# Attention, gated MLP and mixer in one kernel: gate weights prepared during the attention, part of the last matrix stored off the chip, norm steps regrouped

## The chip, the cores and the metric

The kernel runs on one core of one Trainium2 chip. The time is the device time of one execution in microseconds (us). Before the change three runs took 1237.75, 1238.79 and 1238.87 us; their median, 1238.79, is the time before.

## The reference

Three computations follow each other on a batch of 4 (head dimension 64, 8 heads, 1152 positions, so 576 pooled positions of 512 features):

```
attention:  q' = mean over pairs of positions of q          # 4 x 8 x 576 x 64
            p  = softmax(q' k^T / 8);   x = p v              # -> x: 4 x 576 x 512
gated MLP:  h  = gelu(x w_in); u, v = halves of h            # w_in 512 x 1024
            v  = (v - mean) / sqrt(var + 1e-6) * g_ln        # norm over 512 features
            v  = w_sg v + b_sg                               # w_sg 576 x 576, over positions
            x  = x + (u * v) w_out                           # w_out 512 x 512
mixer:      u  = x + (relu(x^T w_tok1) w_tok2)^T             # over positions, 576 -> 256 -> 576
            out = u + relu(u w_ch1) w_ch2                    # over features, 512 -> 1536 -> 512
```

The matrices w_in, w_out, w_tok1, w_tok2, w_ch1 and w_ch2 arrive as 64-bit floats; w_sg arrives in 32 bits. The kernel turns each 64-bit number into a 32-bit one by integer operations on its two halves.

## The kernel before

Every matrix product is done in three passes: each operand is split into a high part, rounded to the type fp32r, and a low part, the rest, and the products high·high, high·low and low·high are summed (`PASSES`, `products`). So each weight needs a conversion and a split before its first use. One *piece* is 128 x 512 numbers (512 KB in 64 bits). `convert` (line 216) loads it into a tile `ws` (two buffers), then does four DVE steps (L239, L243, L247, L252, tile `wz`), two ACT steps before the last of them (L230, L231, tile `wd`), the copy to the high part on POOL (`g_scale`, L210) and the subtraction for the low part on POOL (`sub`, L214). The class `Feed` holds a queue of such pieces; each call of `feed.ops(1)` issues one of the four steps. `Feed.add` appends pieces and starts the first two loads at once; `feed.until(n)` issues whatever is missing until n pieces are done.

The order of all instructions is written out by the program; each engine executes its own list in order.

*Attention* (lines 329 to 701). Sixteen pairs (batch, two heads). For each pair: q and k are loaded, transposed on PE, split (q on L400 to L422, k on L432 and L214); 15 score products `s` (L462) give row maxima on DVE (L469); then 18 transposed score products `sT` (L513), exponentials on ACT (L521) into eight buffers `e`, their running sum `acc` on POOL (L527), the products with v (L536, three column groups at a time), the sum over keys on PE (L549), reciprocal on DVE (L560) and the multiplication into `xT` (L567). The three PSUM banks of `s` and `sT` are shared. The order comes from the class `Plan`: tasks with an engine, a duration, an urgency, predecessors and rings of buffers are scheduled by a list simulation, and the instructions are issued in the resulting order. Sixteen planned DVE tasks call `feed.ops(1)`: with them the four pieces of the second half of w_in (`w0`) are converted during the attention. Loads of q, k and v are two half loads each, the second planned after the first has landed.

*Gated MLP* (`spatial`, from line 717 on). Per batch: V (the v half, three tile pairs, L807), norm (`v_norm`, a list of small steps: a guess, three Newton steps, then for each of five tiles `apply` on DVE and `split` on ACT and POOL), O (output product of the batch before, L915), U (the u half, four blocks, L873), S (the gate over positions, four blocks, L891). A group of products in S is followed by L900 on DVE, L903 on POOL, and a split. The table `HOOKS` says what other work is issued at each point: "0U1e" is batch 0, stage U, block 1, and a letter m, a, e or z for the place within it (in the middle of the products, after them, in the middle of the activation, at its end). The work letters are: c one conversion step, n one norm step, x the split of one tile of x, t and s steps of w_sg's preparation, f a step of closing the attention, w the adding of w_in's first half.

Before the first U stage, w_in's first half (`w1`, four pieces) is converted, since U needs it; during the stages V, U and S of batch 0, w_sg (loaded into `gu` and `b_bc`, lines 757 and 758) is split (L761, ACT and POOL), transposed in both parts by 45 PE transposes (L771), and copied out by ACT (L780, L782); and w_out (`wo`, four pieces) is converted. `bias_load` then loads b_sg and g_ln and scales them on POOL.

*Mixer* (`mixing`, from line 1034 on). F is the last output product; K and Q are the two products over positions (L1088, L1098); M and N are the first block of 256 rows of the two products over features (L1151, L1171), during which `HOOKS` still issues conversions; eight further blocks follow without any. In the last gate stage and in F, K and Q the pieces of w_ch1 (12), w_tok1 and w_tok2 (6) and the first third of w_ch2 (4) are converted; the other eight pieces of w_ch2 are added behind them and are converted in M and N, where `feed.until` makes a product wait for its piece.

Of the kernel before, what the change touches and what calls it, by code (L numbers as in the profile page):

```python
# [27 lines left out]
EARLY_ON = "PP"  # L28
YT = ((), (0, 1, 2), (3, 4), (), (), ())
HOOKS = {  # L30
# [26 lines left out]
class Plan:  # L57
# [20 lines left out]
    def run(self):  # L78
# [21 lines left out]
        while any(todo.values()):  # L100
            best = None
            for eng, ts in todo.items():
                now = free.get(eng, 0.0)
                could = []
                for t in sorted(ts, key=lambda t: t["urgency"])[:90]:
                    at = ready(t)
                    if at is not None:
                        could.append((max(at, now), t["urgency"], t["n"], t))
# [1124 lines left out]
```

## Time and profile before

| | before |
|---|---|
| median of 3 runs | 1238.79 us |
| profiled execution | 1238.36 us |
| span of the profile | 1236.5 us |
| PE busy | 1162.6 us (94%) |
| PE weight loads | 949.0 us (77%) |
| DVE busy | 711.1 us (58%) |
| POOL busy | 611.5 us (49%) |
| ACT busy | 458.5 us (37%) |
| mean granted TensorE clock | 0.978 |

The engines are PE (TensorE), DVE (VectorE), ACT (ScalarE), POOL (GpSimd) and SP (SyncE, which only issues transfers here). The page cuts the span in 40 slices of 30.9 us, one digit each, in tenths of busy time:

```profile
PE   3899999999999999998579999979989999999998
DVE  4767767776676666643976464799987112121111
ACT  1244454445444444453552423434433111111111
POOL 1477877877777777786473414263365111100100
PEclk9899999999999999998789999989998999999999
```

Slices 1 to 18 are the attention, 18 to 25 the four batches of the gated MLP, 26 to 30 the stages F, K, Q, M and N, and the rest the repeating blocks of the mixer. A digit is a mean: a wait shows in PE's row only where it is long against 31 us. Where PE is at 9, other engines' idle time costs nothing.

### The profile page before, as it was taken

Reading aid. Unit: us, or ns where it says so; the run is one execution under the profiler, and the core shown is the slowest. Engines: PE = TensorE matmul, PEld = TensorE weight load, DVE = VectorE, ACT = ScalarE, POOL = GpSimd, SP = SyncE. Lnnn points to the kernel's source line nnn. Section 1 sums busy time; section 2 is a strip of 40 time slices with the busy share of each in tenths; the row PEclk is TensorE's granted clock in tenths of the full one; section 3 lists DMA queues with packets and bytes.
Section 4 is the critical chain, followed back from the end, with each engine's and each line's share of the span. In section 5 each row is a group of like instructions: output and inputs, shape, how many; then the busy total and the mean of one; then the engine's idle time right before and its main releaser. Section 6 shows DMA issues by size and latency. Waiting matters only on the chain.

```text
span 1236.5 us, 22054 instructions
## 1 busy us (share of the span) xinstructions
PE 1162.6 (94%) x9269; PEld 949.0 (77%) x9269; DVE 711.1 (58%) x1017; ACT 458.5 (37%) x847; POOL 611.5 (49%) x452
## 2 busy tenths in 40 slices
PE   3899999999999999998579999979989999999998
PEld 2577777777767777765569898968877899999887
DVE  4767767776676666643976464799987112121111
ACT  1244454445444444453552423434433111111111
POOL 1477877877777777786473414263365111100100
PEclk9899999999999999998789999989998999999999
DMA  6412222222122211002220000023232000000000
GB/s 149 94 40 59 59 56 58 59 59 59 44 55 59 52 46 39 21 1 77 69 62 17 1 1 1 18 69 111 88 100 86 10 17 10 17 18 18 18 17 18
DMA packets 63332, 57.32 MB, mean 46 GB/s; under 512 B 39936, under 2 KB 51968, under 8 KB 63232
## 3 DMA queue, kind: packets, MB, share of 16 engines
q1 hardware_dynamic: 62176, 54.85, 16.3%
q8 instruction: 73, 1.20, 0.4%
q10 hardware_dynamic: 1056, 1.05, 0.3%
q14 instruction: 27, 0.22, 0.1%
HBM read 51.17 MB, written 4.72 MB: 45 GB/s over the span
## 4 chain that ended last, share of the span: by engine, by line
PE 37%; DVE 10%; ACT 1%; issue 1%; POOL 1%; DVEq 0%; ACTq 0%; POOLq 0%
PE psc L1151 11%; PE po L1171 11%; PE pss L891 5%; PE psv L807 3%; DVE wz L247 2%; PE psu L873 2%; PE psz L915 2%; DVE wz L243 2%; DVE wz L252 1%; DVE wz L239 1%; DVE y L214 1%; PE pso L915 1%; PE pu L1163 1%; DVE xT L1102 1%; PE psh L1098 0%
## 5 line engine op out<-in xcount | busy, mean ns | idle before, releaser
L527 POOL TENSOR_TENSOR acc<-acc,e 128x576 f32<-128x576 f32 x224 | 319.7, 1427 | 83.6 <-ACT e L521 65.2
L469 DVE TENSOR_REDUCE mx<-s 128x2 f32<-128x768 f32 (+1 forms) x240 | 225.8, 950 | 115.1 <-PE s L462 111.9
L521 ACT ACTIVATE e<-sT 128x576 f32<-128x576 f32 x288 | 184.2, 652 | 180.0 <-PE sT L513 172.9
L462 PE MATMUL s<-k,q 64*128 64x384 f32 (+1 forms) x1440 | 178.7, 351 | 2.5 <-DVE mx L469 1.9
L513 PE MATMUL sT<-q,k 64*128 64x288 f32 x1728 | 177.3, 307 | 2.6 <-DVE mx L469 1.9
L513 PEld LDWEIGHTS sT<-q,k 64*128 64x128 f32 x1728 | 135.4, 185 | 44.3 <-issue 34.5
L536 PE MATMUL po<-e,vn 128*64 128x288 f32 x1152 | 160.1, 413 | 0.0
L1151 PEld LDWEIGHTS psc<-x,w 128*128 128x128 f32 x1296 | 156.8, 190 | 3.3 <-DVE gc L1078 2.5
L1151 PE MATMUL psc<-x,w 128*128 128x256 f32 x1296 | 157.1, 283 | 2.3 <-DVE gc L1078 2.3
L1171 PE MATMUL po<-w,gc 128*128 128x512 f32 x648 | 156.4, 401 | 2.3 <-POOL w L214 1.7
L1171 PEld LDWEIGHTS po<-w,gc 128*128 128x128 f32 x648 | 121.8, 189 | 32.9 <-POOL w L214 2.5
L462 PEld LDWEIGHTS s<-k,q 64*128 64x128 f32 (+1 forms) x1440 | 116.3, 178 | 19.0 <-issue 10.3
L1077 ACT ACTIVATE gc<-psc 128x256 fp32r<-128x256 f32 x108 | 41.0, 384 | 229.9 <-PE psc L1151 229.9
L536 PEld LDWEIGHTS po<-e,vn 128*64 128x64 f32 x1152 | 75.3, 136 | 60.8 <-issue 20.1
L1078 DVE SCALAR_TENSOR_TENSOR gc<-psc,gc 128x256 fp32r<-128x256 f32 x108 | 45.5, 424 | 100.2 <-ACT gc L1077 100.2
L210 POOL TENSOR_SCALAR x<-xT 128x1024 fp32r<-128x1024 f32 x9 | 9.6, 1069 | 173.6 <-PE psc L1151 173.2
L1178 DVE TENSOR_TENSOR ob<-po,us 128x512 f32<-128x512 f32 x18 | 12.4, 691 | 133.5 <-PE po L1171 133.5
L513 PE MATMUL sT<-nmT,pick 64*128 64x288 f32 x576 | 88.2, 290 | 0.0
L560 DVE RECIPROCAL den<-den 128x288 f32<-128x288 f32 x32 | 62.3, 1947 | 35.6 <-ACT den L556 35.6
L891 PE MATMUL pss<-wsg,vn 128*128 128x288 f32 x448 | 74.6, 315 | 1.8 <-POOL vn L214 1.8
L891 PEld LDWEIGHTS pss<-wsg,vn 128*128 128x128 f32 x448 | 63.9, 193 | 12.0 <-issue 5.4
L873 PE MATMUL psu<-x,w 128*128 128x288 f32 x384 | 56.0, 307 | 10.1 <-issue 8.6
(117 smaller groups left out, 1519.0 us busy)
## 6 DMA issues: line engine op xcount, KB each, us to landing
ws<-in_moe_w_ch_dram SPq DMA_DIRECT2D x24, 512.0 KB, 3.5
qn<-in_q_dram SPq DMA_DIRECT2D x32, 288.0 KB, 4.4
kn<-in_k_dram SPq DMA_DIRECT2D x32, 288.0 KB, 4.1
vn<-in_v_dram SPq DMA_DIRECT2D x32, 288.0 KB, 3.2
out_dram<-ob SPq DMA_DIRECT2D x18, 256.0 KB, 2.0
ws<-in_moe_w_in_dram SPq DMA_DIRECT2D x6, 512.0 KB, 4.7
ws<-in_moe_w_out_dram SPq DMA_DIRECT2D x4, 512.0 KB, 3.5
gu<-in_moe_w_sg_dram SPq DMA_DIRECT2D x1, 1152.0 KB, 5.8
```

The lines of the kernel that those rows point to most:

```text
L462: nc.tensor.matmul(ps[0:m, h, 0:KC], flat(c.q[x])[r, t * P:t * P + m], c.k[y][r, cs], start=(n == 0), stop=(n == 2))
L469: nc.vector.tensor_reduce(out=mx[i % 2][0:m, t, :, g], in_=ps[0:m, :, 0:KC], axis=AX.X, op=ALU.max, negate=True)
L513: nc.tensor.matmul(ps[:, h, 0:TC], left, right, start=(n == 0), stop=(n == 3))
L521: nc.scalar.activation(out=s.e[j], in_=ps[:, :, 0:TC], func=AF.Exp)
L527: eng.tensor_tensor(out=s.acc, in0=s.e[0] if j == 1 else s.acc, in1=s.e[j], op=ALU.add)
L536: nc.tensor.matmul(s.po[D * h:D * h + D, 0:TC], c.vn[:, h, j], s.e[j][:, h], start=(j == 0), stop=(j == J - 1))
L560: nc.vector.reciprocal(out=s.den, in_=s.den)
L873: nc.tensor.matmul(ps[:, ch, 0:TC], wiu[sw][:, cc, fb * P:(fb + 1) * P], X[sx][:, cc, ch * TC:(ch + 1) * TC], start=first, stop=end)
L891: nc.tensor.matmul(ps[:, ch, 0:TC], V[sx][r, ti, db * P:(db + 1) * P], L.ws[sw][r, ti, ch * TC:(ch + 1) * TC], start=first, stop=end)
L1078: nc.vector.scalar_tensor_tensor(out=l_, in0=ps, scalar=0.0, in1=f32(h_), op0=ALU.max, op1=ALU.subtract)
L1151: nc.tensor.matmul(ps, WC1[f // 4][sw][:, cc, (f % 4) * P:(f % 4 + 1) * P], u[sx][:, cc], start=first, stop=end)
L1171: nc.tensor.matmul(pos[tt], g[sx][:, f, tt * P:(tt + 1) * P], WC2[f // 4][sw][:, f % 4], start=(f == 0 and n == 0), stop=(f == NF - 1 and ...
```

## The change

Conversion becomes a class `Piece`, whose steps can be issued by `Feed` as before or as planned tasks. The high part is now copied by ACT, not POOL. A piece has either a destination in SBUF (`dst`) or a place in device memory (`away`): then both parts are written into the piece's own `ws` tile and stored from there.

During the attention the planner now places, besides the four pieces of `w0`, the four of `w1`, the five row tiles of w_sg (unsplit PE transposes, ACT copy, DVE subtraction, stores) and the four pieces of w_out, one of these every 25 us of planned time from 60 on, each load placed behind a score product that is planned 40 us or more earlier. The two half loads of q, k and v are one task, issued together. The last group of products with v of the last pair, with its sums, reciprocal and multiplication, is marked `late` and issued through the f hooks in the first V stage of batch 0. The x splits of the first two tiles move to 40 tasks before the attention's end and, like all x splits of batch 0, to DVE. `w1`, the gate's weights and w_out are fetched back by plain loads when their SBUF space is open, and `bias_load` follows there. The conversions of eight pieces of w_ch2 (blocks 1 and 2 of 0 to 2) are issued by c hooks in the S stages of batches 0, 1 and 2 and stored; they are fetched back ahead of M. Norm steps of batch 0 stand in pairs in its U stage. The t, s and w hooks and the functions they called are gone. In the hooks from the last U stage on, the letters are unchanged.

```
-EARLY_ON = "PP"
+EARLY_ON = "DD"
 HOOKS: ...
+    "0V0a": "f", "0V0z": "f", "0V1a": "f",
+    "0U0a": "nn", "0U0e": "nn", "0U0z": "nn", "0U1a": "nn", "0U1e": "nn", "0U1z": "nn", "0U2a": "nn",
+    c in 0S: 12, in 1S: 12, in 2S: 8
...
+        def high(self):
+            if self.dst:
+                self.parts = self.dst()
+                for x in self.parts[2:]:
+                    g_scale(x, self.z, 1.0)
+            else:
+                self.parts = [self.cut(x) for x in halves(self.s)]
+            nc.scalar.copy(self.parts[0], self.z)
+        def low_part(self):
+            sub(nc.gpsimd, self.parts[1], self.z, f32(self.parts[0]))
+        def send(self, s):
+            nc.sync.dma_start(out=self.away[s], in_=f32(self.parts[s]))
...
+    def fetch(to, x):
+        for s in range(2):
+            nc.sync.dma_start(out=f32(to[s]), in_=x[s])
...
-                first = plan.add("SP", 0.05, lambda: f(i, 0, *a), urgency=u, take=[ring], land=3.5)
-                return first, plan.add("SP", 0.05, lambda: f(i, 1, *a), after=[first], urgency=u,
-                                       land=3.5)
+                return [plan.add("SP", 1.0, lambda: (f(i, 0, *a), f(i, 1, *a)), urgency=u,
+                                 take=[ring], land=4.0)]
...
-        for n in range(4 * CC):
-            plan.add("DVE", 0.75, lambda: feed.ops(1), urgency=20.0 + 26.0 * n)
-        feed.add(*row_block(0, w_in[:, DH:2 * DH], 0))
+        def conversion(x, u):
+            a = plan.add("SP", 0.05, lambda: x.load(nc.sync), after=[mark(u)], urgency=u - 20,
+                         take=["ws"], land=4.0)
+            d1 = plan.add("DVE", 1.2, x.step1, after=[a], urgency=u, take=["wz"])
+            e = plan.add("ACT", 1.4, x.early, after=[a], urgency=u, take=["wd"])
+            d2 = plan.add("DVE", 1.3, x.step2, after=[d1], urgency=u + 0.5)
+            d3 = plan.add("DVE", 1.3, x.step3, after=[d2], urgency=u + 1)
+            d4 = plan.add("DVE", 1.3, x.step4, after=[d3, e], urgency=u + 1.5, ...)
+            h = plan.add("ACT", 0.65, x.high, after=[d4], urgency=u + 2)
+            l_ = plan.add("POOL", 1.4, x.low_part, after=[h], urgency=u + 2, give=[("wz", d1)])
+            if x.away:
+                for s in range(2):
+                    plan.add("SP", 0.05, lambda s=s: x.send(s), after=[h, l_][s:s + 1], ...)
...
+        todo = [w0_piece(j) for j in range(CC)] + col_pieces(A.w1, w_in, 0)
+        todo += list(range(NTT)) + col_pieces(A.wo, w_out, 0)
+        for n, x in enumerate(todo):
+            u = 60.0 + 25.0 * n
+            if isinstance(x, int):
+                gate_weights(x, u)
+            else:
+                conversion(x, u)
+        for n in (1, 2):
+            feed.add(*row_pieces(A.c2[n], w_ch2, 512 * n))
...
         def finish():
-            yield lambda: None
-            yield lambda: None
+            yield lambda: [f() for f in rest[:-2]]
+            yield lambda: [f() for f in rest[-2:]]
             yield lambda: a2.close()
...
+            for s in range(2):
+                nc.sync.dma_start(out=f32(L.ws[s][:, 0:CC]), in_=A.ws[s][:, 0:CC])
+                for r in range(0, P, TAIL):
+                    nc.sync.dma_start(
+                        out=f32(L.ws[s][r:r + TAIL, CC:NTT]), in_=A.ws[s][0:TAIL, CC:NTT])
+            fetch(L.wo, A.wo)
+            bias_load()
...
-            return [lambda ti=ti: x_split(b, ti, nc.gpsimd)
+            return [lambda ti=ti: x_split(b, ti, nc.gpsimd if b else nc.vector)
...
-            feed.add(*row_block(i, w_ch2, 512 * (i - 4)))
+            fetch(W[i], A.c2[i - 4])
```

## Rows read from the trace of the kernel before

**Rows 1.** Stretches (us): busy time and count of each engine, clock, DMA share, GB/s

```profile
120.00:240.00 120.00, 119.39 (x1219) 86.90 (x1219) 84.20 (x110) 58.98 (x109) 93.64 (x64) 1.00 0.22 57
...
652.90:707.60 54.70, 54.70 (x354) 50.05 (x353) 28.34 (x50) 19.09 (x30) 20.81 (x17) 1.00 0.00 1
...
865.00:904.60 39.60, 37.59 (x215) 30.83 (x213) 38.53 (x54) 18.21 (x30) 16.54 (x17) 1.00 0.31 94
...
910.40:953.10 42.70, 38.14 (x226) 32.78 (x225) 36.04 (x49) 15.85 (x30) 25.12 (x22) 0.94 0.27 87
```

**Rows 2.** Timeline of the start: start, length, engine, line, operation [idle before]

```profile
0.73 0.86 SPq L221 DMA_DIRECT2D ws<-in_moe_w_in_dram  x2
...
2.88 1.87 SPq L379 DMA_DIRECT2D vn<-in_v_dram  x2
...
5.35 0.60 SPq L379 DMA_DIRECT2D kn<-in_k_dram  x1
...
15.48 1.09 PE L432 MATMUL pt<-ident,kn 128*128 128x128 f32 x4 [15.48 <-DMA kn<-in_k_dram]
```

**Rows 3.** DMA issues: count, KB each, median us from issue to landing

```profile
ws<-in_moe_w_out_dram SPq DMA_DIRECT2D x4, 512.0 KB, 3.5
gu<-in_moe_w_sg_dram SPq DMA_DIRECT2D x1, 1152.0 KB, 5.8
...
b_bc<-in_moe_w_sg_dram SPq DMA_DIRECT2D x1, 144.0 KB, 5.7
```

**Rows 4.** Groups by line and shape in the attention: busy us, mean ns

```profile
L252 DVE SCALAR_TENSOR_TENSOR wz<-wd,wz 128x512 f32<-128x512 f16 x3 | 6.3, 2097 | 0.0
...
L243 DVE SCALAR_TENSOR_TENSOR wz<-ws,wz 128x512 int32<-128x512 int32 x3 | 4.6, 1523 | 0.0
...
L247 DVE SCALAR_TENSOR_TENSOR wz<-ws,wz 128x512 int32<-128x512 int32 x3 | 2.7, 895 | 0.0
...
L239 DVE TENSOR_SCALAR wz<-ws 128x512 int32<-128x512 int32 x3 | 2.0, 663 | 0.0
```

**Rows 5.** Timeline within the attention, at its end, and at the gate's start

```profile
300.19 0.66 PE L432 MATMUL pt<-ident,kn 128*128 128x128 f32 x4
...
303.53 0.68 DVE L243 SCALAR_TENSOR_TENSOR wz<-ws,wz 128x512 int32<-128x512 int32 x1
...
563.25 3.13 PE L536 MATMUL po<-e,vn 128*64 128x288 f32 x24
...
633.01 19.92 PE L891 MATMUL pss<-wsg,vn 128*128 128x288 f32 x112
```

**Rows 6.** Chain that ended last, in order of time: start, length, what

```profile
689.58 17.99 PE pss L891 x112
707.57 13.99 PE psv L807 x60
...
734.27 12.72 PE psu L873 x96
...
953.30 17.79 PE psc L1151 x144
...
988.77 17.20 PE psc L1151 x144
```

**Rows 7.** Groups by line and shape, 566–653, and the page's groups (L560)

```profile
L820 DVE BATCH_NORM_STATS2 lst<-gv 128x6 f32<-128x512 f32 x5 | 3.4, 681 | 0.2
...
L714 DVE SCALAR_TENSOR_TENSOR gv<-sq,psv 128x1024 f32<-128x1024 f32 x2 | 2.4, 1218 | 1.3 <-ACT sq L713 1.3
...
L713 ACT ACTIVATE sq<-sq 128x1024 f32<-128x1024 f32 x2 | 2.1, 1050 | 1.5 <-DVE sq L708 1.5
...
L560 DVE RECIPROCAL den<-den 128x288 f32<-128x288 f32 x32 | 62.3, 1947 | 35.6 <-ACT den L556 35.6
```

**Rows 8.** Groups by line and shape, 792–905

```profile
L243 DVE SCALAR_TENSOR_TENSOR wz<-ws,wz 128x512 int32<-128x512 int32 x16 | 17.5, 1091 | 0.3
...
L210 POOL TENSOR_SCALAR w<-wz 128x512 fp32r<-128x512 f32 x14 | 9.5, 681 | 38.3 <-DVE wz L252 37.6 <-PE psu L873 0.7
```

More of the change, by code (lines that the diff above doesn't have):

```diff
@@ L67, in ring, with add @@
         self.rings[name] = (n, [])
-    def add(self, eng, dur, fn=None, after=(), urgency=0.0, take=(), give=(), land=0.0):
+    def add(self, eng, dur, fn=None, after=(), urgency=0.0, take=(), give=(), land=0.0,
+            late=False):
         t = dict(eng=eng, dur=dur, fn=fn, after=[x for x in after if x], urgency=urgency,
-                 take=list(take), last=[], land=land, end=None, n=len(self.tasks))
+                 take=list(take), last=[], land=land, late=late, end=None, n=len(self.tasks))
         for ring, owner in give:
@@ L201 @@
         pass
+    A = S0()
     def f32(ap):
@@ L679, in tasks @@
-                r_ = plan.add("DVE", 2.0, lambda x=x: over(i, x), after=[d_], urgency=at + 8)
+                              urgency=at, take=["den"], give=[("tr", s_)], late=last)
+                r_ = plan.add("DVE", 2.0, lambda x=x: over(i, x), after=[d_], urgency=at + 8,
+                              late=last)
                 plan.add("DVE", 0.5, lambda x=x: x_out(i, x), after=[r_, o_], urgency=at + 9,
-                         give=[("os", o_), ("den", d_)])
+                         give=[("os", o_), ("den", d_)], late=last)
@@ new lines, in gate_weights, with load, turn, view @@
+        def gate_weights(ti, u):
+            t0, tn = TT[ti]
+            box = {}
+            def load():
+                box["n"] = ld.tile([P, T], F32, tag="wn", name="wn")
+                nc.sync.dma_start(out=box["n"][0:tn], in_=w_sg[t0:t0 + tn])
+            a = plan.add("SP", 0.05, load, after=[mark(u)], urgency=u - 20, take=["wn"], land=3.5)
+            for g, (i0, i1) in enumerate(((0, 4), (4, 5))):
+                sn = TT[i0][1]
+                def turn(g=g, i0=i0, i1=i1, sn=sn):
+                    box[g] = pt = bank()
+                    box["p", g] = halves(cvp.tile([P, 512], I64, tag="ws", name="wg"))
+                    for i in range(i0, i1):
+                        nc.tensor.transpose(
+                            pt[0:sn, (i - i0) * P:(i - i0) * P + tn],
+                            box["n"][0:tn, i * P:i * P + sn], ident[:tn, :tn])
+                def view(s, g=g, i0=i0, i1=i1, sn=sn):
+                    return box["p", g][s][0:sn, 0:(i1 - i0) * P].rearrange(
+                        "p (i c) -> p i c", c=P)[:, :, 0:tn]
+                def ps(g=g, i0=i0, i1=i1, sn=sn):
+                    return box[g][0:sn, 0:(i1 - i0) * P].rearrange(
+                        "p (i c) -> p i c", c=P)[:, :, 0:tn]
+                def high(g=g, view=view, ps=ps):
+                    nc.scalar.copy(view(0), ps())
+                def low(view=view, ps=ps):
+                    sub(nc.vector, view(1), ps(), f32(view(0)))
+                t_ = plan.add("PE", 0.115 * (i1 - i0), turn, after=[a], urgency=u + g,
+                              take=["tr", "ws"], give=[("wn", a)])
+                h = plan.add("ACT", 0.65, high, after=[t_], urgency=u + g)
+                l_ = plan.add("DVE", 0.7, low, after=[h], urgency=u + g, give=[("tr", t_)])
+                def send(s, i0=i0, i1=i1, sn=sn, view=view):
+                    nc.sync.dma_start(out=A.ws[s][0:sn, i0:i1, t0:t0 + tn], in_=f32(view(s)))
+                for s in range(2):
+                    plan.add("SP", 0.05, lambda s=s, send=send: send(s), after=[h, l_][s:s + 1],
+                             urgency=u + 2 + s, land=3.5, give=[("ws", t_)])
@@ new lines, in attention @@
+        for n, x in enumerate(todo):
[6 more added lines that the diff above has]
+            feed.add(*row_pieces(A.c2[n], w_ch2, 512 * n))
+        early = []
+        rest = []
+        order = plan.run()
+        for n, t in enumerate(order):
+            if n == len(order) - 40:
+                for ti in range(len(EARLY_ON)):
+                    early.append(x_early(ti))
+            if t["late"]:
+                rest.append(t["fn"])
+            elif t["fn"]:
@@ L925, in wo_act @@
             yield
-        splits, pieces, lns, xs_ = [], [], [], []
+        lns, xs_ = [], []
         def hook(name):
@@ L1182, in mixing @@
                 for f in range(NF):
-                    feed.until(io + f + 1)
+                    feed.until(last + f + 1 if f < CC else 0)
                     hook(f"N{f}")
```

231 lines of the change are left out of this document (106 added, 125 removed), and 44 rows, old and new, of the table HOOKS.

## The prediction

> **What bounds the kernel now.** I read the page first: TensorE is busy 94% of the span and every other engine under 60%, so only a stretch in which PE idles, or PE work taken out, can move the end. Its slices show PE idle at the start, in slices 18 to 21, and a little in 26 and 29. The table by stretches separates the regimes. In the attention PE has no gap to speak of (119.4 of 120 us), POOL is at 78%, DVE at 70% [rows 1]. Between the attention's last products (563.25) and the first of the gate (633.01) lie 69.8 us [rows 5] in which PE computes little; that is the hole of slices 18 to 20. In 865–905 DVE is busy 38.5 of 39.6 us and PE 37.6, and in 910–953 PE computes 38.1 of 42.7 us [rows 1]: here DVE sets the pace. From 953 on a loop of 35.5 us repeats [rows 6] with nothing to gain.
>
> The page's profiled execution took 1238.36 us, 1.9 more than its span and 0.4 less than the median of three runs, 1238.79. I sum against 1238.4.
>
> **Start.** Before, two loads of 512 KB of weights are first on SP's queue, then one half each of q and k, two halves of v, and only then the second halves; PE waits 15.48 us for the last half of k [rows 2]. Ahead of that went 1024 KB of weights and 576 each of q, k and v, 2752 KB in the 14.75 us since the first issue: 187 KB a us. After the change each weight load is tied to a later score product, and both halves of q and of k go first: 1152 KB, 6.2 us, landing near 7 to 8. Nothing else stands between: **−7.5 us**. Bounds: −4 if the planner puts v between again, −10 if the steps up to the first scores overlap better once q lands before k.
>
> **Attention.** Twelve pieces of 64-bit weights are converted here instead of four, and the 576x576 gate matrix is turned in 25 transposes. Four transposes take at most 0.66 us in the middle of the attention [rows 5], so 25 cost PE 25 × 0.165 = 4 us; PE has no gap to hide them in. The old transposes of that matrix go from the hole, where PE idled anyway. A conversion's four DVE steps average 0.66 + 1.52 + 0.90 + 2.10 = 5.2 us here [rows 4]; eight more pieces make 41 us, and ten subtractions (no row of their own; the nearest, half-size and full-size splits, lie between 0.2 and 0.8) 5 us. Over the 425 us in which the planner spreads the pieces, DVE goes from 70% to some 80%, and near 90% while a piece is in work. DVE's queue is in order: behind a conversion step stand the row maxima, and a score bank is freed only by its row maximum; with three banks for both score products PE can bear little. In the trace the reciprocal of 1.95 us [rows 7] sits in the same queue twice per pair, and PE still shows no gap, so one late step is mostly absorbed. Nothing shows 42 of them. Bounds: 0 (all absorbed) to 46 us (each lands on PE). I take 3 us, near the row that I have. Sum **+7**.
>
> A two-input step takes 0.68 us when it runs freely [rows 5] and 0.9 to 2.1 on average here. The Trainium skill (SBUF — State Buffer, "Who interferes with whom") says that a DVE instruction with two SBUF inputs and a GpSimd instruction reading SBUF exclude one another, whoever issued first keeping the port; the rows agree. The rule speaks against this change, since POOL too is held up: by it 24 added steps of 0.69 us would cost POOL 17 us in 425, still short of its bound, and the sum stands.
>
> SP also issues more: two stores for each piece kept off the chip and four for each gate tile, each waiting for ACT, DVE or POOL, and the loads of q, k and v queue behind them. Those loads are asked for some ten us ahead, and 512 KB lands in 3.5 us [rows 3], so I cost this at nothing; without that lead it would be a wait of a few us per piece, within the bound of 46.
>
> **From attention to gate.** Let E = 564.8, halfway through the last 24 products of probabilities and v [rows 5]; the second twelve are now late, with their sums and division, placed behind the first product group of V. PE's work up to the gate is then V 14.0 us, the late part 1.6 + 0.5, U 12.7 [rows 6]: 28.8, so 593.6 if nothing waits. Something does: DVE's queue now also carries the x splits and the late reciprocal. In DVE's order: V's first pair is ready at E+8.3 (ACT takes the late copies first); square 1.0 on ACT, 1.2 on DVE, tanh 1.05 on ACT, 1.2 on DVE, statistics 1.7, reciprocal 1.95 [rows 7] and the multiply, 0.8 by estimate: E+17.3; the tail tile's split 0.8; the second pair 5.2 in the same way; splits of tiles 0 and 1, 0.7 each like the other one-tile steps, around a step of the last tile: E+25.5. U's products need that last split after the first 1.1 us of U, which could start at E+16.1, so PE loses 8.3 us. Then POOL: five subtractions, 1.3 to 1.5 us each by my estimate, follow in U, the last some 2 us later than the gate wants it. And the bias: POOL's queue now holds the scaling of b_bc ahead of these five, and b_bc is loaded behind the returned gate and output matrices on SP's queue. A 144 KB load issued just behind the 1152 KB one took 5.7 us, as long as the large one [rows 3], so one in front delays. The slope from 512 to 1152 KB is 640 KB in 2.3 us, 278 KB a us. The second gate half can follow only the late multiply (E+17.3): with 3776 KB to go, b_bc lands at about E+33 and POOL is past it at E+34.4; the first subtraction is due about E+32.5. I add 2 us. Gate at 593.6 + 8.3 + 2 + 2 = 605.9 against 633.0: 27. The first gate stage ran 19.92 us against 17.99 later [rows 5, 6]; it should gain those 2, and I take 2 off for the new gaps, as the gaps before it cost as much. Sum **−27**. Bounds: −41 with no waits, −15 if the loads come back at 199 KB a us (1152 KB in 5.8).
>
> **Gate stages.** 32 conversion steps (eight pieces of the last matrix) are new in the first three gate stages. In the second batch DVE is busy 28 of 54.7 us [rows 1], PE without a gap; twelve steps of about 1.2 us give the four gate groups (18 us) some 23 us of DVE work, and the backlog runs into V and O, which have room; three PSUM buffers cover it. **+1**; bounds 0 to +12.
>
> **The stretch bound by DVE, 792–905.** The hooks are the same, and 88 steps (22 pieces) fall to it against 90 before: no gain from that. But the copy of the high part goes from POOL to ACT. A step of L243 averages 1.09 us here against 0.68 free, 6.6 us over its 16 [rows 8]; with L247 alike, 13. The copies, 9.5 us of POOL [rows 8], I hold to cause a third: **−4**. By the skill's port rule every copy could cost DVE its full length, 22 × 0.62 = 13.6 us. Bounds 0 to −9.
>
> **First block of the last two products, 910–953.** 30 conversion steps before, none after; instead four loads of 1 MB, 15 us at 278 KB a us, wanted some 24 us after they can be issued. Its PE work is one loop of 35.5 us (988.77 − 953.30, [rows 6]) against 42.7 [rows 1]: **−7**; bounds −4 to −7.2.
>
> Sum: −7.5 + 7 − 27 + 1 − 4 − 7 = −37.5, so **1201 us**.
>
> **Rivals.**
> Slower: the added DVE steps land on PE through the three score banks. At their full 46 us instead of 3 the time is 1244; it decides from 40 us above what I take, 0.95 us for each of 42 instructions. For it: no gap on PE in the attention, POOL and DVE near their limits. Against: the longer reciprocal hardly shows. 5%.
> The gate's weights and the bias come back late: at 199 KB a us, with both gate halves behind the multiply, POOL's last subtraction comes 12 us later: 1213. For it: one queue; against: the slope of 278. 15%.
> The eight pieces don't fit the gate stages: a buffer holds its piece until the store has landed, so load, four steps, copy, subtraction and store (over 12 us with 3.5 for each transfer) run in turn on two buffers, DVE stands at a load, and PE runs out of PSUM: +10, 1211. 8%.
> Nearly no waits remain: no loss in the DVE chain to U (−8), attention at +4 (−3), −9 instead of −4 in the DVE-bound stretch: 1185. 15%.
>
> **Chances.** The forecast 55%, its own range 1190 to 1212; 2% that parts cancel to no change. The range 1185 to 1219 holds the forecast, most of the second and third rival and half of the last. About 0.2%, 2.5 us, is what can be told from no change here: faster 93%, same 2%, slower 5%.
>
> **What would show it.** The first transpose near 8 us instead of 15.5. An attention some 7 us longer from there to its last score product; if row maxima release PE for tens of us, it is the slower rival. U's first product waiting on an x split, POOL's b_bc scaling directly ahead of the vn subtractions, and the first gate product 27 us nearer to the attention's end. No wz step after 905, and the first po product without a POOL release. I am wrong if the hole stays over 55 us, or if the attention grows by over 20.

## The result and the profile after

The changed kernel takes 1223.18 us (median of 4 runs, 1220.27 to 1224.05) against 1238.38 (4 runs): a ratio of 0.9873, 95% interval 0.9856 to 0.9891. It is faster, but by 15.2 us and not by the 37.5 forecast, and its time lies 4 us above the upper end of the range, 1219. The profiled execution took 1224.05 us, with a span of 1222.3 us against 1236.5 before. The account below is made between the two spans, from the starts of PE's product groups in the two timelines. One trace of each kernel is kept; the one of the changed kernel is the slowest of its four executions.

| stretch | before | after | change | forecast |
|---|---|---|---|---|
| start to the first sT product | 51.45 | 45.27 | −6.2 | −7.5 |
| attention, first to last sT | 511.4 | 522.2 | +10.8 | +7 |
| last sT to the first gate product | 70.1 | 42.0 | −28.1 | −27 |
| first gate product to V of batch 1 | 19.8 | 18.3 | −1.4 | 0 |
| V of batch 1 to U of batch 3 | 135.9 | 145.5 | +9.6 | +1 |
| U of batch 3 to the first psc product (M) | 121.7 | 131.1 | +9.3 | −4 |
| first block of the last two products | 42.7 | 34.9 | −7.8 | −7 |
| the other eight blocks | 283.4 | 283.0 | −0.4 | 0 |
| sum | 1236.5 | 1222.3 | −14.2 | −37.5 |

From the profile page of the changed kernel, 40 slices of 30.6 us:

```profile
PE   5899999999999999999889999879999999999998
...
DVE  5688888887767779864756575879861112121111
```

The hole of before is down to an 8 in slices 20 and 21. What has come instead is an 8 and a 7 in slices 26 and 27: there begins the stretch that the forecast called bound by DVE. DVE's row no longer has the three 9 in a run that it had (slices 27 to 29), and PE idles although DVE is not full.

The start of the changed kernel, in the timeline (it answers to [rows 2]):

```profile
0.73 1.20 SPq L415 DMA_DIRECT2D qn<-in_q_dram  x2
1.99 2.25 SPq L425 DMA_DIRECT2D kn<-in_k_dram  x2
4.28 2.88 SPq L425 DMA_DIRECT2D vn<-in_v_dram  x4
...
8.70 0.66 PE L478 MATMUL pt<-ident,kn 128*128 128x128 f32 x2 [8.70 <-DMA kn<-in_k_dram]
```

Stretches of the changed kernel (busy time and count of PE, PEld, DVE, ACT and POOL, granted clock, DMA share, GB/s), the first, second and last answering to those of [rows 1]:

```profile
120.00:240.00 120.00, 116.06 (x1169) 83.97 (x1168) 105.94 (x121) 62.22 (x114) 103.13 (x66) 1.00 0.32 79
627.90:688.60 60.70, 57.61 (x354) 52.01 (x354) 36.92 (x61) 23.05 (x36) 22.10 (x18) 0.94 0.15 50
...
904.40:939.30 34.90, 34.90 (x226) 31.60 (x225) 8.01 (x17) 6.20 (x15) 8.15 (x5) 1.00 0.30 121
```

The first row is new in kind: PE had 0.6 us of gaps in these 120 us of the attention, now 3.9, with DVE at 88% and POOL at 86%. In the second the same 354 matrix instructions of batch 1 take 60.7 us instead of 54.7, at a clock of 0.94 instead of 1.00. In the last PE has no gap any more, as forecast.

PE's timeline after, from the attention's end to batch 1 (it answers to [rows 5]; in brackets the idle time before, and what ended it):

```profile
569.46 5.78 PE L916 MATMUL psv<-w,xe 128*128 128x512 f32 x24
...
588.01 1.20 PE L916 MATMUL psv<-w,x 128*128 128x512 f32 x4 [2.40 <-DVE x L220]
591.74 2.29 PE L982 MATMUL psu<-x,w 128*128 128x288 f32 x8 [2.52 <-ACT x L363]
595.00 14.68 PE L982 MATMUL psu<-x,w 128*128 128x288 f32 x88 [0.97 <-DVE x L220]
609.52 18.51 PE L1000 MATMUL pss<-wsg,vn 128*128 128x288 f32 x112
627.86 8.56 PE L916 MATMUL psv<-w,x 128*128 128x512 f32 x36
639.51 5.49 PE L916 MATMUL psv<-w,x 128*128 128x512 f32 x12 [3.09 <-ACT x L363]
```

The first gate product comes 40.1 us after the attention's end (609.52 − 569.46), where the forecast had 41.1. The last row is where the gain begins to go: PE waits 3.1 us, and the 12 products behind the wait take 5.49 us where the same 12 in batch 2 (757.77) take 3.06. The clock had fallen: its mean over 627.86 to 644.79 is 0.82, made of 0.99 ahead of the wait and 0.50, the lower of the two levels (1.2 and 2.4 GHz), behind it:

```profile
639.50:644.80 5.30, 5.29 (x13) 4.13 (x14) 2.86 (x3) 2.24 (x3) 2.80 (x4) 0.50 0.42 135
```

Why PE waits there is read from the other engines, 634 to 640:

```profile
634.45 1.74 POOL L1012 TENSOR_TENSOR gt<-gt,gu 128x576 f32<-128x576 f32 x1 [3.44 <-DVE gt L1009]
636.22 0.67 ACT L1014 CAST g<-gt 128x576 fp32r<-128x576 f32 x1 [3.18 <-POOL gt L1012]
636.93 0.76 DVE L220 TENSOR_TENSOR g<-gt,g 128x576 fp32r<-128x576 f32 x1 [2.03 <-ACT g L1014]
637.60 0.68 DVE L271 SCALAR_TENSOR_TENSOR wz<-wd,wz 128x512 f32<-128x512 f16 x1
638.32 0.62 ACT L281 CAST ws<-wz 128x512 fp32r<-128x512 f32 x1 [1.42 <-DVE wz L271]
638.84 0.92 ACT L363 CAST x<-xT 128x512 fp32r<-128x512 f32 x2
```

Read upwards: the x split that V waits for (L363) stands in ACT's queue behind the high copy of a converted piece (L281); that waits for step 4 on DVE (L271); that stands behind the gate's difference (L220); and that waits for POOL by way of ACT. x itself, written by the attention, was ready all along. The same knot appears in F, around 810:

```profile
810.07 1.71 POOL L1012 TENSOR_TENSOR gt<-gt,gu 128x576 f32<-128x576 f32 x1 [1.83 <-DVE gt L1009]
810.56 1.77 DVE L265 SCALAR_TENSOR_TENSOR wz<-ws,wz 128x512 int32<-128x512 int32 x1
812.43 0.69 DVE L271 SCALAR_TENSOR_TENSOR wz<-wd,wz 128x512 f32<-128x512 f16 x1
813.16 0.62 ACT L281 CAST x<-wz 128x512 fp32r<-128x512 f32 x1 [4.39 <-DVE wz L271]
813.68 0.67 ACT L1014 CAST g<-gt 128x576 fp32r<-128x576 f32 x1
814.38 1.35 DVE L220 TENSOR_TENSOR g<-gt,g 128x576 fp32r<-128x576 f32 x1 [1.26 <-ACT g L1014]
814.40 0.85 PE L1024 MATMUL pso<-g,wo 128*128 128x288 f32 x2 [4.39 <-ACT g L1014]
```

gt is done at 811.78, but ACT has been waiting in L281 for DVE's step 4 and turns to g only at 813.68, 1.9 us late. DVE in turn waits for g (1.26 us), so its next steps are late, and with them ACT's next copy. PE waits 4.39 us. PE waited for g in F before the change too, 6.0 us in all; now it is 8.0 (experiment 1).

### The profile page after: what moved, and what is told of

Same layout as the page of the kernel before. It is cut to its first block, busy times and chain, and to the rows that moved or that the text cites. A ratio compares the mean times of both kernels' runs of the same rounds, so it can differ in the third digit from the quotient of the medians.

```text
span 1222.3 us, 22129 instructions
## 1 busy us (share of the span) xinstructions
PE 1164.0 (95%) x9249; PEld 946.8 (77%) x9249; DVE 731.7 (60%) x1032; ACT 470.8 (39%) x868; POOL 576.8 (47%) x398
## 4 chain that ended last, share of the span: by engine, by line
PE 66%; DVE 19%; POOL 6%; ACT 4%; issue 4%; DMA 1%; SPq 0%; POOLq 0%; DVEq 0%; ACTq 0%
PE psc L1244 13%; PE po L1264 12%; PE sT L559 11%; PE s L508 10%; PE po L582 10%; POOL acc L573 3%; DVE mx L515 3%; PE pss L1000 2%; PE pt L478 2%; DVE wz L265 2%; PE psu L982 2%; DVE wz L259 2%; DVE wz L271 1%; POOL gt L1012 1%; PE pt L595 1%
## 5 line engine op out<-in xcount | busy, mean ns | idle before, releaser
L573 POOL TENSOR_TENSOR acc<-acc,e 128x576 f32<-128x576 f32 x224 | 328.5, 1466 | 62.0 <-ACT e L567 43.4
L1264 PE MATMUL po<-w,gc 128*128 128x512 f32 x648 | 153.3, 396 | 0.0
L1264 PEld LDWEIGHTS po<-w,gc 128*128 128x128 f32 x648 | 120.8, 188 | 28.8
L573 POOL TENSOR_TENSOR acc<-e 128x576 f32<-128x576 f32 x32 | 46.2, 1444 | 41.5 <-ACT e L567 41.5
```

The costliest lines, as they stand in the source:

```text
L573: eng.tensor_tensor(out=s.acc, in0=s.e[0] if j == 1 else s.acc, in1=s.e[j], op=ALU.add)
L1264: nc.tensor.matmul(pos[tt], g[sx][:, f, tt * P:(tt + 1) * P], WC2[f // 4][sw][:, f % 4], start=(f == 0 and n == 0), stop=(f == NF - 1 and ...
```

## The experiments

Beside each, the kernel before ran again (its medians were 1237.8 to 1238.7 us), and ratios are to that. Times are medians; stretches are read from the one trace that was kept of each. The attention's length repeats well: in the six other traces with the attention of the changed kernel (experiment 1, both kernels of 2, experiments 4, 5 and 9) it takes 522.2 or 522.3 us, as in the first.

**1. The copies back on POOL** (`e1_pool_copy`: only for the pieces that are converted behind the attention).

```
-            nc.scalar.copy(self.parts[0], self.z)
+            if pool:
+                g_scale(self.parts[0], self.z, 1.0)
+            else:
+                nc.scalar.copy(self.parts[0], self.z)
```

> The changed kernel with the copy of the high part on POOL again, as before the change, for the pieces that the hooks issue (gate stages, F to Q); the attention's conversions keep the ACT copy. Theory: the copy on ACT stands in ACT's queue waiting for the fourth DVE step, and the gate's and the relu's activations wait behind it; that costs the 8 to 10 us that the changed kernel loses between the last U stage and M, and part of the loss in the gate stages. Then the time falls from 1223 to 1211-1215, and PE's waits for ACT g and ACT r shrink to 6 and under 1 us. Rival (the step of the prediction): the copy on POOL costs DVE some 4 us through the port that the two share, so the time rises to 1225-1228.

Measured 1215.18 us (ratio 0.9821, 0.9806 to 0.9835), 8 us less than the changed kernel: the first theory, at the upper edge of its 1211 to 1215, and far from the rival's 1225 to 1228. Stretch U of batch 3 to M, first the kernel with POOL's copies, then the changed kernel:

```profile
772.09:896.24 124.15, 113.72 (x691) 99.64 (x689) 115.79 (x154) 54.86 (x90) 60.82 (x55) 0.95 0.26 79
```

```profile
773.38:904.43 131.05, 114.61 (x690) 99.21 (x689) 110.35 (x154) 64.42 (x111) 46.32 (x34) 0.95 0.25 75
```

With ACT's copies DVE is busy 5.4 us less for the same 154 instructions, and yet the stretch is 6.9 us longer. What ended PE's longest waits in it, in the kernel before and in the changed one (total us, times, longest):

```profile
PE pso L915 <- ACT g L905: 6.0, 2, 4.8
...
PE psh L1098 <- ACT r L1077: 0.4, 1, 0.4
```

```profile
PE pso L1024 <- ACT g L1014: 8.0, 2, 4.4
...
PE psh L1191 <- ACT r L1170: 2.7, 4, 1.0
```

In experiment 1 they are back at 6.0 and 0.4. So already before the change ACT ended 6.4 of the 11.0 us in which PE stood in this stretch, although DVE was the busiest engine; the changed kernel makes that 10.7 of 16.4. The difference is clear of the spread between traces: the stretch takes 128.9 to 136.1 us in seven other traces with ACT's copies in it (experiments 2, 4, 6, 7, 8's first and both of 10), and 121.9 to 125.2 in three others with POOL's (2's second, 5 and 8's second). The gate's stages gain little by it: V of batch 1 to U of batch 3 takes 144.2 us instead of 145.5, and PE's waits for x splits there come to 4.7 us instead of 3.5. The same knot as above in this run, in F: g starts right behind gt (POOL, no copy in ACT's queue).

```profile
808.15 0.67 ACT L1017 CAST g<-gt 128x576 fp32r<-128x576 f32 x1 [2.97 <-POOL gt L1015]
...
809.62 0.98 POOL L216 TENSOR_SCALAR x<-wz 128x512 fp32r<-128x512 f32 x1 [1.51 <-DVE wz L271]
```

**2. The eight pieces late again** (`e2_c2_late`), and **the same with POOL's copies** (`e8_pool_late`).

```
-        for n in (1, 2):
-            feed.add(*row_pieces(A.c2[n], w_ch2, 512 * n))
...
-            fetch(W[i], A.c2[i - 4])
+            feed.add(*row_block(i, w_ch2, 512 * (i - 4)))
```

> The changed kernel with the eight pieces of the last matrix converted in M and N again, as before the change; the gate stages hold no conversions of them. Theory: the 32 steps in the gate stages cost the 9 us that are lost between the second V stage and the last U stage, M and N cost 7 to 8 more than in the changed kernel, so the time is 1221-1224 with the first V-to-U losses gone. Rival: the gate stages lose their 9 us because they now come earlier than the x splits on ACT and POOL, whatever is converted there; then the loss stays and the time is 1229-1232.

> The changed kernel with the copy on POOL for the hooks' pieces and the eight pieces converted in M and N again. Theory: the two effects add, 8 us from the copy and about 1 from the place of the eight pieces, so 1213-1216, and the place of the eight pieces alone is worth nothing as it is hooked in the change. Rival: with POOL's copy the eight pieces cost less in the gate stages, and undoing them costs 5 us or more: 1219-1222.

Measured 1222.13 (ratio 0.9875, 0.986 to 0.989) and 1214.0 us (0.9803, 0.9787 to 0.9819): in either form the eight pieces are worth nothing as they are hooked, against the changed kernel and against experiment 1. They save 6.7 us in the first block (41.5 us without, 34.9 with) and cost 9.6 in the gate's stages. Without them V of batch 1 to U of batch 3 takes to the hundredth what it took before, 135.91 us, with PE busy for all of it:

```profile
627.86:763.77 135.91, 135.91 (x863) 123.91 (x861) 73.02 (x132) 43.06 (x65) 41.41 (x35) 1.00 0.00 1
```

**3. The start alone** (`e3_start_only`: the kernel before with both halves of a load together and the weights' loads tied to a score product).

```
-        feed.add(*row_block(0, w_in[:, DH:2 * DH], 0))
+        start = plan.add("SP", 0.05, lambda: feed.add(...), after=[marks[0]], ...)
```

> The kernel before with only the order of its first loads changed: the weight loads follow a later score product, and both halves of q, k and v are asked for together. Theory: the first transpose moves from 15.5 to 8.7 us and the whole of the attention with it, so 6 to 7 us are gained, 1231.5-1232.5. Rival: the gain at the start is given back in the attention, where the order that the planner finds changes too: 1236-1239.

Measured 1230.95 us (0.995, 0.9933 to 0.9966): −6.9. The first sT comes at 44.2, and the attention takes 511.7 us, so the change of the loads costs it nothing, and the 10.5 us that it has on top in the changed kernel come from what else the change puts there:

```profile
44.20:555.90 511.70, 509.05 (x5185) 369.96 (x5183) 346.23 (x440) 250.52 (x457) 399.34 (x272) 1.00 0.20 51
```

**4. The bias ahead of the fetches** (`e4_bias_first`: `bias_load()` moved to the front of them).

> The changed kernel with the bias loaded ahead of the gate's weights and of the output matrix. Theory: nothing changes (1222-1224), because POOL's scaling of the bias was over at 601.1 us in the changed kernel and the first subtraction behind it was not ready before 603.8. Rival (the prediction's term of 2 us, and its second rival): the subtractions start earlier and the gate with them, 1219-1221.

Measured 1222.77 us (0.9879, 0.9865 to 0.9894): no effect. POOL's scaling of the bias now runs at 576.1 instead of 600.3, and the subtractions begin at 602.4, 34.3 us behind the attention's end as before (603.8, 34.4): the bias was not what they waited for.

**5. Other points for the 32 steps** (`e5_hooks_moved`: experiment 1, and two steps at the middle of each activation in S of batches 0 to 2, one at that of each U of batches 1 and 2, instead of the points of the change).

```
+for _k in list(HOOKS):
+    if _k[1] == "S" and _k[0] in "012":
+        HOOKS[_k] = HOOKS[_k].replace("c", "")
...
+        HOOKS[f"{_b}S{_g}e"] = HOOKS.get(f"{_b}S{_g}e", "") + "cc"
+        if _b != "0":
+            HOOKS[f"{_b}U{_g}e"] = HOOKS.get(f"{_b}U{_g}e", "") + "c"
```

> The changed kernel with the copy on POOL for the hooks' pieces, and the 32 steps of the eight pieces moved: two at each e point of the twelve gate groups of batches 0 to 2, where DVE waits for POOL and ACT anyway, and one at each e point of the U groups of batches 1 and 2. Theory: the 9.6 us that the eight pieces cost between the second V stage and the last U stage come from steps placed where DVE's queue holds up the bias step, the split of g and behind them the x splits; with the steps in DVE's own waits at most 3 us remain, so the time is 1207-1210. Rival: it is the amount of work on DVE, ACT and POOL in these stages, wherever it is put, and the time stays at 1213-1216, as with the copy alone.

Measured **1209.07 us** (1208.84 to 1211.37; ratio 0.977, 0.9756 to 0.9785), the best of all runs and better than both kernels. The gate's stages, V of batch 1 to U of batch 3:

```profile
626.85:763.81 136.96, 136.41 (x862) 123.96 (x861) 102.12 (x160) 50.73 (x78) 60.63 (x50) 1.00 0.18 59
```

1.05 us over the 135.91 without any step, although DVE has more instructions in this stretch than after (160 against 157). So the stages do have room for the 32 steps; it was their points that cost, not their number. Against experiment 1, which has the same copies on POOL and the old points, the stretch gains 7.2 us (144.2 to 137.0). The other 1.4 of the 8.6 us against the changed kernel are not clear: with the old points and ACT's copies the stretch takes 144.1 to 145.5 us from trace to trace. The new points with ACT's copies were not tried.

**6. Steps 2 and 3 doubled in the attention** (`e6_steps_doubled`: 24 more DVE steps, planned).

> The changed kernel with the second and third DVE step of each of the twelve conversions in the attention issued twice (both give the same bits again), and known to the planner: 24 more DVE steps there. Theory: the 42 added DVE steps cost PE some 6 us, 0.15 us each, so 24 more cost 3 to 5 us: 1226-1228. Rival (the slower rival of the prediction, coming in): with DVE near 90% the steps now land on PE with most of their length, 24 of about 1.2 us: 1240-1252. Second rival: DVE costs PE nothing and the attention grew through PE's transposes alone: 1222-1224.

**7. The gate's transposes doubled** (`e7_turns_doubled`: `for i in [*range(i0, i1)] * 2`, planned).

> The changed kernel with the 25 transposes of the gate matrix in the attention done twice, and known to the planner. Theory: PE has no gap there, so 25 more cost 3 to 4.5 us: 1226-1228. Rival: they fit between PE's waits for row maxima: 1222-1224.

Measured 1226.6 us (0.9905, 0.9891 to 0.992) and 1222.98 (0.9879, 0.9864 to 0.9894). From first to last sT the attention takes 525.3 us with the steps doubled, 3.1 more: 0.13 us a step, so the slower rival (0.95 us a step) falls. With the transposes doubled it is 523.1, 0.9 more: my theory missed, 25 more transposes are nearly free on top of the first 25. PE's busy time grows by 2.4 us (514.57 to 516.97), its idle time falls by 1.5 (7.6 to 6.1). What the first 25 cost is another question (experiment 10).

**8. ACT's steps doubled** (`e9_act_doubled`), and **22 of them given to DVE** (`e11_copies_on_dve`, on top of experiment 5).

```
-            h = plan.add("ACT", 0.65, x.high, after=[d4], urgency=u + 2)
+            h = plan.add("DVE", 0.7, lambda: x.high(vector=True), after=[d4],
+                         urgency=u + 2)
...
-                h = plan.add("ACT", 0.65, high, after=[t_], urgency=u + g)
+                h = plan.add("DVE", 0.7, high, after=[t_], urgency=u + g)
```

> The changed kernel, with ScalarE's added steps of the attention each issued once more: the first absolute value of the 12 pieces, the copy of their high part, and the eviction of the 10 transposed gate tiles, 34 instructions in all (about 20 us of ScalarE), and the planner told of it. The attention, first to last score product, was 522.2 us after and 511.7 us with the change of the start alone: 10.5 us for the added work, of which the doubled DVE steps (3.1 us for 24, so 5.5 us for 42) and the doubled transposes (0.9 us) leave some 4 us without an owner. Theory: they belong to ScalarE's 34 added steps, which stand in the queue of the exponentials: the attention takes 525 to 527 us, the kernel 1226 to 1229 us. Rival: ScalarE has room (busy about half of the attention) and the exponentials lose nothing: the attention stays at 522 to 523 us, the kernel at 1222 to 1225 us, and the 4 us stay open.

> The kernel with the copies on POOL and 32 DVE steps moved into the gate's stages (1209.1 us; attention 522 us from first to last score product), and in the attention the 12 high copies of the pieces and the 10 evictions of the transposed gate tiles taken off ScalarE and given to DVE, with the planner told. Theory: a step added to the attention on ScalarE costs 0.27 us (9.2 us for the 34 doubled ones), one on DVE 0.13 us (3.1 us for 24): 22 steps moved are worth 22 x 0.14 = 3 us, up to the 6 us of ScalarE's price alone; the attention takes 516 to 519 us, the kernel 1203 to 1206 us. Rival: DVE, now busy 415 of 522 us, takes their place in front of the attention's own steps (or its copies hold POOL's sums up, on which ScalarE's exponentials wait): attention 522 us or more, kernel 1208 to 1212 us.

Both missed. With ACT's 34 steps doubled the kernel takes 1236.01 us (0.9988, 0.9977 to 0.9999), more than either theory; the attention 531.4 us, 9.2 more, or 0.27 us a step. Only half of that is waiting: PE's busy time, for the same products, is 4.5 us longer, at a mean clock of 0.99 instead of 1.00. The rest of the 12.8 us lies behind the attention, where nothing was changed: in the profiled execution (1239.25 us, the slowest of the ten) U of batch 3 to M takes 136.1 us instead of 131.1, at a clock of 0.92 instead of 0.95. Why, I did not find. Given to DVE, 22 steps did not give that back: 1211.54 us (0.9782, 0.9769 to 0.9795), with the attention at 527.6 us, 5.3 longer than in experiment 5. The two attentions, of experiment 8's second kernel and of the changed kernel:

```profile
44.80:572.40 527.60, 517.62 (x5210) 373.50 (x5209) 425.36 (x506) 261.36 (x474) 416.86 (x276) 1.00 0.28 73
```

```profile
45.30:567.50 522.20, 514.57 (x5209) 373.08 (x5206) 405.56 (x484) 270.42 (x496) 415.88 (x276) 1.00 0.29 73
```

**9. Four more pieces kept off the chip** (`e10_more_away`: experiment 5 with the first third of the last matrix too, 16 steps more, and one further point in each of the four O blocks of batches 1 and 2).

```
+            HOOKS[f"{_b}O{_g}e"] = HOOKS.get(f"{_b}O{_g}e", "") + "c"
...
-        for n in (1, 2):
+        for n in (1, 2, 0):
```

> The kernel with the copies on POOL and 32 DVE steps moved into the gate's stages (1209.1 us), and besides four more pieces of the last matrix kept off the chip: its first third too is converted beside the gate, by one more DVE step at each point behind an O stage of batches 1 and 2, and fetched before the first mixing product. 16 steps leave the stretch from the last U of batch 3 to the mixing's end (889.0 - U3 now). Theory: DVE is still that stretch's bound, so 16 steps of about 0.8 us are worth up to 12 us there, and the O points give 4 to 8 of them back: 1202 to 1206 us. Rival: the O points cost as much as the stretch gains (DVE's steps there stand in front of what the U stage waits for), or ScalarE's relu bounds the mixing: 1208 to 1211 us.

Measured 1217.03 us (0.9824, 0.9805 to 0.9843), 8 more than experiment 5 and worse than either theory. The edit does not do what the theory says: eight points take eight steps, two pieces of the four. They cost nothing; V of batch 1 to U of batch 3 takes 137.0 us, as in experiment 5, with 168 DVE instructions instead of 160:

```profile
627.37:764.40 137.03, 136.42 (x863) 124.00 (x861) 110.10 (x168) 52.93 (x80) 64.24 (x53) 1.00 0.22 74
```

The other two pieces stay in the queue, and the c hooks of batch 3, which in experiment 5 find the queue empty until U, take them up: four steps in its V and O stages, so that a piece's copy and subtraction stand on POOL ahead of U's x split. U of batch 3 waits for that split and runs on at a lower clock (20 products take 2.81 us ahead of the wait, the next 76 take 12.98, against 10.33 after):

```profile
771.14 12.98 PE L996 MATMUL psu<-x,w 128*128 128x288 f32 x76 [3.94 <-POOL x L231]
```

U of batch 3 to M takes 133.9 us instead of 125.2, the whole loss. So it is again a matter of points, and whether all 16 steps at good points would gain is open.

**10. The attention's added work in two parts** (`e12_gate_once`: a fifth of the gate's transposes, evictions and differences; `e13_pieces_once`: a quarter of the eight added pieces; the stores stay).

> The changed kernel with only the first of the five row blocks of the gate's weights transposed and split beside the attention; its two parts are sent to all five places, so the transfers out stay and the values in the other four places are wrong. Left out: 20 transposes, 8 evictions on ScalarE, 8 differences on DVE. Theory (the attention's 10.5 us are the sum of many small waits, each added step costing as the doublings showed: 0.27 us on ScalarE, 0.13 on DVE, 0.04 a transpose): 8 x 0.27 + 8 x 0.13 + 20 x 0.04 = 4 us back; the attention, 522.2 us, takes 517 to 519 us and the kernel 1218 to 1220 us. Rival (the attention's length is set by the planner's order, and what an edit does to it has little to do with the steps' number; moving 22 steps from ScalarE to DVE made it 5 us longer): under 1.5 us back, or more than 6; 1221 us or more, or under 1217 us.

> The changed kernel with one piece in four of w1's and wo's halves converted beside the attention (2 instead of 8), its two parts sent to all four places, so the transfers out stay and the values in six places are wrong. Left out: 24 DVE steps, 18 steps on ScalarE, 6 on POOL, 6 loads. Theory (small waits that add up, at the prices of the doublings): 24 x 0.13 + 18 x 0.27 = 8 us back, of the 10.5 us that the added work costs; the attention takes 514 to 516 us and the kernel 1214 to 1217 us. Rival (the planner's order, not the number of steps): the attention stays over 519 us and the kernel over 1219 us.

Measured 1215.99 us (0.9829, 0.9813 to 0.9846) and 1216.59 (0.9829, 0.9814 to 0.9844). First the attention without four fifths of the gate's work, then without three quarters of the pieces:

```profile
43.00:561.70 518.70, 511.57 (x5187) 372.00 (x5186) 399.95 (x476) 267.54 (x488) 416.72 (x276) 1.00 0.27 72
```

```profile
45.10:560.20 515.10, 512.73 (x5208) 373.68 (x5207) 368.91 (x460) 259.94 (x478) 402.05 (x270) 1.00 0.26 68
```

3.5 and 7.1 us shorter than after, 4 and 8 expected: the attention's loss belongs to both parts, two thirds to the pieces, and by its length neither rival holds: the planner's order does not explain these two (the 5.3 us of experiment 8's second kernel stay unexplained). The two parts cost in different ways. Without that part of the gate's work PE's busy time falls by 3.0 us (514.57 to 511.57) and its idle time by 0.5; without those pieces PE's busy time falls by 1.8 and its idle time by 5.3 (7.6 to 2.4). What is left over experiment 3's attention without those pieces, 3.4 us, is PE's busy time alone (509.05 to 512.73, 3.7 us), which fits the 25 transposes. The first kernel's time is lower than the attention explains (its first sT is 2.3 us earlier, and another 3.8 us come behind the attention); its time alone would have spoken for the rival, its attention does not.

## Why the prediction was wrong, and where it was right

**Right.** The start: the first transpose moved from 15.48 to 8.70 where I said "near 7 to 8", and experiment 3 has −6.9 against −7.5. The hole: −28.1 against −27, and PE does wait for an x split ahead of V's last products and of U (2.4, 2.5 and 1.0 us) and for the late part (0.4). But here part of the agreement is luck. These waits are 6.3 us of the 40.1 in place of 12.3: 8.3 for U's split, 2 for POOL and 2 for the bias. The gate (609.52) starts right behind U, without a wait for POOL, and experiment 4 shows that the bias held nothing up, so the last two were for nothing. In exchange PE's own work took 33.8 us instead of 28.8: U runs behind the waits at a granted clock of 0.73 and takes 17.8 us, waits included, instead of 12.7, and the sum has no term for that. The first block of the last products: −7.8 against −7.

**The DVE-bound stretch (−4, measured +9.3)** is the step that failed worst. I priced the move of the high copy by what it takes from POOL and DVE and asked nothing of the engine that receives it. The DVE gain did come. Steps by line in the stretch, after (773 to 895) and then with the copies on POOL (772 to 896):

```profile
L265 DVE SCALAR_TENSOR_TENSOR wz<-ws,wz 128x512 int32<-128x512 int32 x16 | 17.0, 1061 | 0.3
L259 DVE SCALAR_TENSOR_TENSOR wz<-ws,wz 128x512 int32<-128x512 int32 x16 | 13.1, 816 | 0.3
```

```profile
L259 DVE SCALAR_TENSOR_TENSOR wz<-ws,wz 128x512 int32<-128x512 int32 x18 | 18.8, 1046 | 0.4
L265 DVE SCALAR_TENSOR_TENSOR wz<-ws,wz 128x512 int32<-128x512 int32 x17 | 18.4, 1081 | 0.4
```

Without POOL's copies step 2 (L259) takes 816 ns instead of 1046 and step 1 (L253) 460 instead of 664; the 5.4 us that DVE is less busy lie within my bounds of 0 to 9. For step 2, which reads two inputs from SBUF, the Trainium skill (SBUF — State Buffer, "Who interferes with whom") has this: such a step contends with a GpSimd instruction that reads SBUF. Step 3 (L265) reads two as well and hardly changes, 1061 and 1081 ns; why the gain falls on the other two, no run shows. But ACT executes in order, and its queue holds g and relu, on which PE waits, behind a copy that waits for DVE. So an engine that was busy 43% of this stretch before (52.9 of 121.7 us) ends 10.7 us of PE's waits instead of 6.4. Experiment 1 gives 6.9 of the 9.3 back. What is left, 2.4, is about PE's busy time, 113.7 against 110.8 us for the same products, at a clock of 0.95 instead of 0.97.

**The gate's stages (+1, measured +9.6)** are the second step that failed; 5.7 of the 9.6 us are waits, 3.9 slower products (PE busy 139.84 against 135.91 us, clock 0.98). I compared the sum of DVE's work with its room, and "three PSUM buffers cover it". The sum was right: experiment 5 puts as many steps there for 1.05 us. What I left out is who stands behind a step at its point: at the points of the change a step lies between a gate group's POOL result and its split, and on ACT and POOL the piece's copy and subtraction lie ahead of the x splits of the next V stage. None of the rows that I read shows a conversion step in these stages, and I should have followed the queue of each point, as I did for the chain to U. My bound of +12 held it, and so did the third rival's +10 in size; its mechanism, the turn-around of two buffers, was not the one: PE's waits there end on ACT's x splits (3.5 us) and DVE's gv (2.1 us), and DVE stands for ACT and PE, not for a load.

**The attention (+7, measured +10.8).** The mechanism was right: nearly all of PE's waits there end on DVE. What was mis-sized is the conversions. I gave the transposes 4 us, the 42 DVE steps 3 and ACT's steps nothing. By experiment 10 the gate's part, most of it the transposes' own time on PE, costs some 3.5 us, near the 4 (3.5 came back with four fifths of it left out), and the eight pieces 7 (7.1 with three quarters left out). Experiment 7's 0.9 us is the price of 25 transposes more, which PE's waits partly take in, and not of the first 25. The prices of the doublings (0.13 us for a DVE step, 0.27 for one on ACT) hold on top of the full load in the same way: for 42 DVE steps and the 38 that ACT got here (24 for eight pieces, 10 for the gate, 4 copies that were POOL's) they would add up to 16 us, more than the 10.5 there are. A conversion's four steps together took a little less than I forecast from [rows 4], though two of them (L253 and L265) took longer:

```profile
L271 DVE SCALAR_TENSOR_TENSOR wz<-wd,wz 128x512 f32<-128x512 f16 x12 | 18.8, 1563 | 0.1
L259 DVE SCALAR_TENSOR_TENSOR wz<-ws,wz 128x512 int32<-128x512 int32 x12 | 14.8, 1234 | 0.1
L265 DVE SCALAR_TENSOR_TENSOR wz<-ws,wz 128x512 int32<-128x512 int32 x12 | 13.7, 1145 | 0.0
L253 DVE TENSOR_SCALAR wz<-ws 128x512 int32<-128x512 int32 x12 | 10.0, 833 | 1.8 <-DMA ws<-in_moe_w_out_dram 1.8
```

That is 4.8 us a piece against 5.2. How the price splits between DVE and ACT stays open: by the doublings a step on DVE is half as dear, but 22 steps moved from ACT to DVE made the attention 5.3 us longer.

**The sum.** Of the 23.3 us between forecast and result 13.3 are the DVE-bound stretch, 8.6 the gate's stages, 3.8 the attention and 1.3 the start; the other terms give 3.7 back. With the copies on POOL and the steps at other points the same change gives 29 us (1209.07).

## What to carry to other kernels

Before work is moved to an idle engine, write down that engine's queue at the place: what the moved instruction waits for, and what stands behind it that the critical engine waits for. An engine's idle share says nothing of that, nor does a high busy share make an engine the one that PE waits for: list what ends PE's waits in the stretch. The number of added steps can be right for a stretch and their points still cost 7 us; move the points before giving the idea up. In this attention, where PE is full and two more engines are near 80%, a step more cost 0.13 us on DVE and 0.27 on ACT, though neither is the busiest engine. And doubling a piece of work prices more of it, not what is there; for that, leave it out.

## What the runs showed of the hardware

25 more PE transposes lengthened the attention by 0.9 us, although PE is busy 98.5% of it (514.6 of 522.2 us). PE's busy time grew by 2.4 us and its idle time fell from 7.6 to 6.1: a PE that looks full still had waits inside, and the transposes filled some of them.

What a stall costs behind itself varies. The same 3.1 us wait for the x split, at the same place, stands in seven traces; the 12 products after it took 3.36 us (experiment 10's first kernel, granted clock 1.00 there), 4.27 to 4.63 (experiments 4, 6, 7, 8's first and 10's second; 0.62 in experiment 7) and 5.49 (the changed kernel, 0.50), against 3.06 in batch 2, behind a wait of 0.46 us. So the stall cost between 0.3 and 2.4 us on top of itself. Without it (experiment 5) the clock in this stretch is 1.00.
